# Holding back the load of batch 1's x until the first piece of batch 0's x has landed

## The chip, the core and the metric

The kernel runs on one core of a Trainium2 chip. The metric is the device time of one execution in microseconds (us); the time of the kernel before is 225.44 us, the median of 3 runs (225.27 to 225.44).

The core has five engines with instruction queues of their own, each in order: TensorE (PE in the profile; its weight loads are listed apart as PEld), VectorE (DVE), ScalarE (ACT), GpSimd (POOL) and SyncE (SP), which here only issues transfers. Transfers between the chip's memory and the on-chip memory are carried out by 16 DMA engines. Transfers issued by SP go through the queue that the profile calls q1, those issued by ACT through q10, and those issued by POOL through q0.

## The reference

```python
# x: (8, 8, 512, 64), state: (8, 8, 32, 64); B, H, S, D and Ns = 32
scores = scale * np.matmul(x, state.transpose(0, 1, 3, 2))
a = softmax(scores)                        # over the 32 states
xread = np.matmul(a, state)
scores2 = scale * np.matmul(state, x.transpose(0, 1, 3, 2))
a2 = softmax(scores2)                      # over the 512 tokens
sread = np.matmul(a2, x)
h = concatenate([xread, sread], axis=2)    # then (batch, position) x (head, D) = 4352 x 512
gate = 1 / (1 + np.exp(-(h @ w_gate)))     # 512 x 1536
val = h @ w_val
out = (gate * val) @ w_out                 # 1536 x 512
```

## The kernel before

The work goes batch by batch (8 batches of x). For a batch, x arrives as 32-bit floats in the tile `xf` (128 partitions x 8 heads x 4 x 64; 1 MB), is cast to bfloat16 (`xb`), is transposed (`xT`), and is multiplied with the state for the scores (`S_mm`). ACT takes the exponentials (`S_exp`), DVE sums the rows (`n_sum`, line 139) and inverts the sums, the normalized scores (`ab`) are transposed (`aT`), and the product with `SW` (the state times the two input weights) gives gate and value (`gv_mm`, line 288). A tanh on ACT and a product on DVE make `glu`, and `out_mm` (line 319) multiplies by the output weight. The second attention (`sr_mm`, `sr_fin`) shares the exponentials; its results `XS` are collected and go through the feed-forward part last.

The order of the instructions on each engine is the order in which the code is written (`manual_schedule`): batches 0 and 1 are interleaved by hand from line 392 on, the others follow in a loop. An engine whose next instruction waits holds up everything written for it further down. The change works in the first 11 us of the hand-written part. What stands there, in the order of the code:

- `load_s(0)` (line 392) issues the state of batches 0 and 1 on ACT; `load_x(0, nc.sync, 4)` (line 393) issues x of batch 0 on SP in four transfers of two heads each, 256 KB; `load_x(1, nc.sync, 4)` (line 394) does the same for batch 1, with no wait. The next thing on SP is a DMA transpose much later.
- POOL: makes the identity matrix, casts heads 0 and 1 of batch 0 (line 404), casts the state (`cast_s`), issues three weight transfers of 256 KB, then `gate` (line 431), a copy of one element per partition that waits for heads 6 and 7 of batch 0 and so holds back the further weight transfers; then two of these, the cast of heads 6 and 7 of batch 1 (line 445), and `at_Eb` (line 132), a cast of the exponentials.
- DVE: fills constants, casts heads 2 and 3 of batch 0 (line 406), copies the padded state and the transposed x out of PSUM (lines 382 and 108), casts heads 2 and 3 of batch 1 (line 429), casts heads 4 and 5 of batch 1 (line 439), and then sums the rows (`n_sum(0, 1)`, line 440). From there to `sr_fin(0)` (line 476) it goes on with sums, reciprocals, copies and products of both batches.
- ACT: casts heads 6 and 7, then 4 and 5 of batch 0 (lines 413 and 416), with a copy of a transposed tile, casts heads 0 and 1 of batch 1 (line 436), and takes the exponentials (`S_exp(0, 1)`, line 438).
- PE: runs matmuls on constants (`warm`) while it waits, transposes x, and computes scores. `aT_mm(1, OU)` (line 483) writes to the PSUM tile that `sr_fin(0)` on DVE has to leave first.

All casts of x stand at line 91 in the profile, all transfers of x at line 74.

Of the kernel before, what the change touches and what calls it, by code (L numbers as in the profile page):

```python
# [8 lines left out]
FP = mybir.dt.float32  # L9
# [7 lines left out]
def kernel(  # L17
# [14 lines left out]
    nc = tc.nc  # L32
    B, H, S, D = x.shape
# [10 lines left out]
    stg = ctx.enter_context(tc.tile_pool(name="stg", bufs=3))  # L44
# [20 lines left out]
    xfs, xbs, xTs = {}, {}, {}  # L65
# [2 lines left out]


    def load_x(b, eng, parts=1):  # L70
        xf = xfs[b] = stg.tile((128, H, 4, D), FP, name="xf")
        v, n = x[b].rearrange("h (p c) d -> p h c d", c=4), H // parts
        for i in range(parts):
            eng.dma_start(xf[:, n * i:n * i + n], v[:, n * i:n * i + n])  # L74

    def load_w(w, lo, n):
        src = (moe_w_gate, moe_w_val)[w].rearrange("(k p) n -> p k n", p=128)
        nc.gpsimd.dma_start((wg, wv)[w][:, :, lo:lo + n], src[:, :, lo:lo + n])
# [9 lines left out]
    def cast_x(b, cp, lo, n):  # L88
        if b not in xbs:
            xbs[b] = xp.tile((128, 4, H, D), BF, name="xb")  # L90
        cp(xbs[b].rearrange("p c h d -> p h c d")[:, lo:lo + n], xfs[b][:, lo:lo + n])  # L91
# [257 lines left out]
    def warm(n, place):  # L349

        ps = place[0].tile((128, 512), FP, name="warm", tag=place[1])
        for _ in range(n):
            nc.tensor.matmul(ps[:, :128], ones[:, 0], ones[:, 0], start=True, stop=True)  # L353
# [37 lines left out]

    load_s(0, nc.scalar)
    load_x(0, nc.sync, 4)
    load_x(1, nc.sync, 4)
    make_identity(nc, ident)
    for e in range(2):
        nc.vector.memset(ones[:, e, e * 64:e * 64 + 64], 1.0)
# [3 lines left out]
    pre = wp.tile((128, 2), FP, name="pre")  # L401
    nc.scalar.activation(pre[:, 0:1], ones[:, 0, 0:1], AF.Exp)

    cast_x(0, pool, 0, 2)
    warm(12, OU)
    cast_x(0, vec, 2, 2)
# [105 lines left out]
    load_sb(3)  # L512
    load_sb(1)
    load_x(2, nc.gpsimd, 2)
    p_tok(1)
    sw_cp(1, 1024, 0, 1, act)
# [221 lines left out]
```

## Time and profile before

| what | us |
|---|---|
| median of 3 runs | 225.44 |
| the profiled execution | 226.03 |
| its span, first to last instruction | 224.2 |
| PE busy | 217.0 |
| DVE busy | 140.7 |
| ACT busy | 127.6 |
| POOL busy | 48.8 |

The durations in the text come from the one profiled execution. The span is what lies between its first and its last instruction; some 1.8 us lie around it. All times of the trace count from the start of the span.

A line of a group in the profile names the line of the code, the engine, the operation, what it writes and reads (output <- inputs, shapes), and how often; then busy time, mean duration of one in ns, and how long the engine stood idle before these instructions and for whom. A line of the timeline gives start and duration in us, engine, line, operation, tiles and count, and in brackets the idle time before it with what ended it. The chain of waits follows the work that ended last back to what released it, and lists the pieces in order of time. A line on transfers gives what was loaded, the issuing engine, count, size of one, and the median time from issue to landing.

### The profile page before, as it was taken

The page shows a single profiled execution, that of the slowest core. Times are in us where ns is not written, and L with a number is a line of the kernel's source. Part 1 is how long each engine was busy: PE and PEld are TensorE (multiplying, and loading weights), DVE is VectorE, ACT ScalarE, POOL GpSimd, SP SyncE. Part 2 cuts the span into 40 slices and gives each one's busy share as a digit, 9 for nine tenths or more (in the row PEclk, how much of TensorE's full clock was granted, in tenths as well). Part 3 has the DMA queues.
Part 4 walks back from the last instruction along what each step waited for, and adds up shares of the span by engine and source line. Part 5 has one row for each costly group of instructions (what it writes and reads, how often), then busy time and mean ns, then how long its engine had stood idle before and what let it go on. Part 6 is the DMA issues. An engine that isn't in the chain of part 4 may idle for free.

```text
span 224.2 us, 4791 instructions
## 1 busy us (share of the span) xinstructions
PE 217.0 (97%) x1859; PEld 111.2 (50%) x1859; DVE 140.7 (63%) x248; ACT 127.6 (57%) x239; POOL 48.8 (22%) x85
## 2 busy tenths in 40 slices
PE   7789999999999999999999999999999999999994
PEld 6654444444444545454444454454445444466744
DVE  3599897779368756885488648864787434422311
ACT  2587885645676557656675667556755444423311
POOL 3799560362041004200240006000200000000001
PEclk9999999999999999999999999999999999999999
DMA  6999989753898352627362521253122111111114
GB/s 188 289 201 206 280 130 179 114 193 78 147 292 274 71 151 76 219 59 126 100 225 50 121 96 61 44 81 117 47 78 66 50 50 47 67 73 48 50 26 114
DMA packets 38566, 27.37 MB, mean 122 GB/s; under 512 B 21168, under 2 KB 33840, under 8 KB 38544
## 3 DMA queue, kind: packets, MB, share of 16 engines
q1 hardware_dynamic: 31392, 19.74, 32.5%
q0 software_dynamic: 6864, 7.14, 17.6%
q8 instruction: 14, 0.23, 0.4%
q10 hardware_dynamic: 288, 0.20, 0.3%
q14 instruction: 8, 0.07, 0.1%
HBM read 18.35 MB, written 8.91 MB: 122 GB/s over the span
## 4 chain that ended last, share of the span: by engine, by line
PE 91%; DVE 3%; DMA 2%; ACT 1%; SPq 1%; issue 0%
PE outp L319 38%; PE gvp L288 37%; PE swp L236 5%; PE gvp L291 5%; DMA xf<-in_x_dram 2%; PE srp L213 1%; PE Sp L121 1%; PE outp L339 1%; DVE rs L139 1%; PE srp L210 1%; SPq L74 1%; DVE ab L173 1%; DVE ri L141 0%; DVE r L218 0%; PE xTp L105 0%; PE warm L353 0%
## 5 line engine op out<-in xcount | busy, mean ns | idle before, releaser
L303 DVE SCALAR_TENSOR_TENSOR glu<-th,gvp 128x512 bf16<-128x512 f32 (+1 forms) x108 | 69.9, 655 | 64.0 <-ACT th L298 48.7
L319 PE MATMUL outp<-wo,glu 128*128 128x512 bf16 x396 | 98.2, 379 | 0.0
L288 PE MATMUL gvp<-aT,SW 128*128 128x512 bf16 x384 | 96.3, 379 | 0.3 <-DVE aT L190 0.2
L298 ACT ACTIVATE th<-gvp 128x512 f32<-128x512 f32 (+1 forms) x108 | 61.8, 574 | 60.6 <-PE gvp L288 49.2
L288 PEld LDWEIGHTS <-SW 128*128 128x128 bf16 x384 | 36.3, 98 | 44.7 <-issue 3.1
L319 PEld LDWEIGHTS <-glu 128*128 128x128 bf16 x396 | 37.4, 98 | 40.8 <-issue 0.4
L274 ACT CAST SW<-swp 128x512 bf16<-128x512 f32 x70 | 38.8, 586 | 4.7 <-PE swp L236 3.3
L132 POOL CAST Eb<-E 128x256 bf16<-128x256 f32 x32 | 11.5, 407 | 89.9 <-ACT E L126 89.9
L323 ACT ACTIVATE res<-outp 128x512 f32<-128x512 f32 x33 | 19.7, 597 | 17.6 <-PE outp L319 17.6
L274 DVE CAST SW<-swp 128x512 bf16<-128x512 f32 x26 | 17.1, 683 | 1.6 <-PE swp L236 1.4
L91 POOL CAST xb<-xf 128x1024 bf16<-128x1024 f32 (+1 forms) x13 | 13.8, 1093 | 12.1 <-DMA xf<-in_x_dram 10.7
L330 POOL DMA_DIRECT2D out_dram<-res x2 | 1.1, 542 | 60.0 <-ACT res L323 60.0
L147 DVE TENSOR_REDUCE E<-E 128x128 f32<-128x512 f32 x12 | 12.4, 1035 | 0.0
L139 DVE TENSOR_REDUCE rs<-E 128x16 f32<-128x512 f32 x16 | 10.8, 676 | 1.3 <-ACT E L126 1.3
L126 ACT ACTIVATE E<-Sp 128x512 f32<-128x512 f32 x16 | 9.6, 604 | 2.4 <-PE Sp L121 2.4
L173 DVE TENSOR_TENSOR ab<-E,ri 128x512 bf16<-128x512 f32 x12 | 9.6, 804 | 0.0
L236 PE MATMUL swp<-wg,sTc 64*32 64x512 bf16 (+1 forms) x192 | 8.4, 328 | 0.0
L236 PEld LDWEIGHTS <-sTc 64*32 64x32 bf16 x384 | 4.5, 91 | 7.4 <-issue 4.7
L218 DVE RECIPROCAL r<-srp 128x128 f32<-128x128 f32 x8 | 7.6, 950 | 0.0
L121 PEld LDWEIGHTS <-xT 128*128 128x128 bf16 x128 | 5.5, 98 | 4.0 <-DVE xT L108 1.0
L236 PE MATMUL swp<-wv,sTc 64*32 64x512 bf16 (+1 forms) x192 | 7.4, 322 | 0.0
L291 PE MATMUL gvp<-XS,wg 128*128 128x256 bf16 x48 | 7.2, 273 | 0.0
(64 smaller groups left out, 122.0 us busy)
## 6 DMA issues: line engine op xcount, KB each, us to landing
out_dram<-res SPq DMA_DIRECT2D x31, 256.0 KB, 2.6
xf<-in_x_dram SPq DMA_DIRECT2D x12, 256.0 KB, 4.5
xf<-in_x_dram SPq DMA_DIRECT2D x3, 1024.0 KB, 6.8
wo<-in_moe_w_out_dram POOLq DMA_DIRECT2D x3, 512.0 KB, 5.9
wg<-in_moe_w_gate_dram POOLq DMA_DIRECT2D x2, 512.0 KB, 9.2
wv<-in_moe_w_val_dram POOLq DMA_DIRECT2D x2, 512.0 KB, 10.8
xf<-in_x_dram POOLq DMA_DIRECT2D x2, 512.0 KB, 10.4
xf<-in_x_dram POOLq DMA_DIRECT2D x1, 1024.0 KB, 9.2
```

The source lines that it names most:

```text
L91: cp(xbs[b].rearrange("p c h d -> p h c d")[:, lo:lo + n], xfs[b][:, lo:lo + n])
L139: nc.vector.tensor_reduce(rs, halfE(b, i), AX.X, ALU.add)
L147: nc.vector.tensor_reduce(held["E4", b][:, e].rearrange("p j n -> p (j n)"), E1s[b][:, :, e].rearrange("p c j n -> p (j n) c"), AX.X, ALU.add)
L173: eng.tensor_tensor(abs_[b].rearrange("p c e (j n) -> p (c e) j n", n=Ns)[:, ce, 2 * i:2 * i + 2], halfE(b, i)[:, ce], ri[:, ce].unsqueeze ...
L236: nc.tensor.matmul(pss[e][j * Ns:(j + 1) * Ns, o:o + n], sTc[rows, b, j] if b > 1 else sTz[rows, b, j, e], (wg, wv)[w][rows, j, lo:lo + n] ...
L274: cp(*sw_left.pop((b, lo, w, e)))
L288: nc.tensor.matmul(ps, SWs[b][:, g, w, fs], aTs[b][:, :, g], start=(g == 0), stop=(g == 1))
L291: nc.tensor.matmul(ps, (wg, wv)[w][:, j, fs], XS[:, j], start=(j == 0), stop=(j == 3))
L298: nc.scalar.activation(th, held["gv", b, f][0], AF.Tanh, scale=0.5)
L303: nc.vector.scalar_tensor_tensor(glus[b][:, f], held["th", b, f], 1.0, held["gv", b, f][1], ALU.add, ALU.mult)
L319: nc.tensor.matmul(ops[b, c], glus[b][:, f, c * 128:(c + 1) * 128], wo[:, f], start=(f == 0), stop=(f == NF - 1))
L323: nc.scalar.activation(res, ops[b, c], AF.Copy, scale=0.5)
```

## The change

`load_x` no longer makes its tile if it exists already. A new helper, `hold_x(b, a)`, makes the tile for batch b and lets POOL copy one element per partition of batch a's tile into it. Since the element belongs to heads 0 and 1 of batch a, the copy waits for the first transfer of batch a; and since it writes where the first transfer of batch b is going to write, SP waits for the copy before it issues this transfer. The load of batch 1 is moved behind the constants, follows `hold_x(1, 0)`, and is cut in two transfers of four heads, 512 KB each, where it was cut in four. The copy stands on POOL ahead of the cast of heads 0 and 1 of batch 0. The casts and all that follows stand in the order in which they stood.

```diff
     def load_x(b, eng, parts=1):
-        xf = xfs[b] = stg.tile((128, H, 4, D), FP, name="xf")
+        if b not in xfs:
+            xfs[b] = stg.tile((128, H, 4, D), FP, name="xf")
+        xf = xfs[b]
         v, n = x[b].rearrange("h (p c) d -> p h c d", c=4), H // parts
         for i in range(parts):
             eng.dma_start(xf[:, n * i:n * i + n], v[:, n * i:n * i + n])
+
+    def hold_x(b, a):
+
+        xfs[b] = stg.tile((128, H, 4, D), FP, name="xf")
+        nc.gpsimd.tensor_copy(xfs[b][:, 0, 0, 0:1], xfs[a][:, 0, 0, 0:1])
...
     load_s(0, nc.scalar)
     load_x(0, nc.sync, 4)
-    load_x(1, nc.sync, 4)
     make_identity(nc, ident)
...
     nc.scalar.activation(pre[:, 0:1], ones[:, 0, 0:1], AF.Exp)
 
+    hold_x(1, 0)
+    load_x(1, nc.sync, 2)
     cast_x(0, pool, 0, 2)
```

## The prediction

> **What bounds the kernel now.** The page's first two parts say that TensorE (PE) is the bound, but not evenly. The columns are busy time, share of the span, instructions; in the second row one digit is 5.6 us.
>
> ```profile
> PE 217.0 (97%) x1859; PEld 111.2 (50%) x1859; DVE 140.7 (63%) x248; ACT 127.6 (57%) x239; POOL 48.8 (22%) x85
> ...
> PE   7789999999999999999999999999999999999994
> ```
>
> PE has holes in the first four slices only. I asked next for PE's waits from 18 us to the end: the answer lists none. So from 18 us on PE cannot make up what it loses before, and what the change does to the moment at which that stretch begins is what it does to the end, nearly one for one. The edit works in the first 11 us, so I read the chain of waits from 7 to 18.6 us (start, length, what):
>
> ```profile
> 2.27 5.24 DMA xf<-in_x_dram
> ...
> 7.53 0.63 ACT xb L91
> ...
> 10.09 0.60 ACT E L126
> ...
> 10.71 0.70 DVE rs L139
> ...
> 17.55 0.30 DVE XS L226
> 17.85 0.04 issue
> 17.90 0.61 PE aTp L180 x8
> ```
>
> The chain starts at the last quarter of batch 0's x (issued at 2.27, landed at 7.51), goes through ACT's cast, transposes and scores to the exponentials at 10.09, and from 10.71 to 17.85 it lies on VectorE (DVE) without a gap. DVE is strictly in order, so whatever starts the row sums at 10.71 (line 139) sets the end. The timeline shows what stands ahead of them:
>
> ```profile
> 4.22 0.61 POOL L91 CAST xb<-xf 128x512 bf16<-128x512 f32 x1 [2.91 <-DMA xf<-in_x_dram]
> ...
> 9.12 0.62 ACT L91 CAST xb<-xf 128x512 bf16<-128x512 f32 x1
> ...
> 9.50 0.75 DVE L91 CAST xb<-xf 128x512 bf16<-128x512 f32 x2
> ...
> 10.38 0.62 POOL L91 CAST xb<-xf 128x512 bf16<-128x512 f32 x1 [1.22 <-DMA xf<-in_x_dram]
> 10.71 0.69 DVE L139 TENSOR_REDUCE rs<-E 128x16 f32<-128x512 f32 x1 [0.46 <-ACT E L126]
> ```
>
> The casts at 9.12 and later are batch 1's. On DVE the cast of heads 4 and 5 of batch 1 (line 439) stands right before the row sums (line 440); now it is done at 10.25 and DVE then waits 0.46 us for ACT. The only cast of batch 1 that waits for its data is POOL's, of the last quarter, which is there at 10.38.
>
> **The change, part by part.**
> *The copy.* One more POOL instruction of one element per partition. The nearest row is the gate's copy (line 82): 0.19 us. It waits for batch 0's first quarter, for which POOL's cast at 4.22 waits anyway, so it adds no wait on POOL, but everything behind it moves by 0.19: that cast, the state's cast (4.78), the weight transfers (from 5.12), the gate (7.56). The cast feeds PE and DVE, which then idle 1.23 us until 8.21 and 2.05 us until 9.16: hidden. Of the weights, the first that PE waits for is wait-bound by 0.2 us at 15.92, and its work is not on the chain, which is DVE's there: hidden, and if not, 0.2.
>
> *The issue on SP.* Eight issues of about 0.47 us each become four, a wait, and two. Now batch 1's go out from 2.78 to 4.79. After: the quarter lands at 4.2, the copy runs from 4.22 to 4.41, SP wakes at about 4.45 (an estimate: 0.04 after its releaser, as in its other rows), issues the halves at 4.45 and 4.95. The next thing on SP is a transpose at 31.68, so nothing behind the wait suffers.
>
> *When batch 1 lands.* This is the disputed number. Now its four quarters are issued at 2.78 to 4.3 and take 5.5, 5.7, 5.9 and 6.0 us, since they stand in line behind batch 0; the last is there at 10.3. After, 1 MB is issued from 4.45. The trace has no 1 MB in two halves, so I bound it by the nearest rows. Above: 1 MB in one transfer, issued at 86.44 and at 59.41, took 6.6 and 6.8 us (a third took 9.0, among output stores). Near: batch 7's x in four quarters, issued from 110.03; its last quarter, issued about 112.1, took 4.0, so 6.1 us from the first issue. Below: the first quarter alone takes 3.4, and if the other 768 KB followed at the 367 GB/s that the windows show from 3 to 4 us, that is 3.4 + 2.1 = 5.5 us. So batch 1 is complete between 4.45 + 5.5 = 9.95 and 4.45 + 6.8 = 11.25. I take 6.25, between the two nearest rows (6.1 and 6.6) and nearer to the one that is cut in pieces: 10.7.
>
> Why it isn't just as early as now: now the 2 MB run through one queue without a break. After, batch 0's data is almost through when batch 1's halves are issued, and a transfer of this queue moves nothing for its first 1.4 us (issued at 0.74; the windows show 15 GB/s up to 2.00), then ramps up: after the issue at 110.03, 47 GB/s in 111.5 to 112.0, 332 in the next microsecond.
>
> *What that costs.* Heads 4 to 7 now come as one piece. DVE's cast of heads 4 and 5 can start 0.05 after the landing and takes 0.42, the row sums start 0.02 later: 10.7 + 0.49 = 11.19 in place of 10.71, so **+0.48 us**. POOL's cast of heads 6 and 7 moves from 10.38 to 10.75 and its next work (line 132) from 11.23 to about 11.4; POOL's part of the chain ends at 17.44, some 0.4 us before DVE's, so this hides. The first half must be there for ACT's cast at 9.12, behind which the exponentials wait; they need it by 9.4. One quarter takes 3.4 and a second 0.7 more at full rate, so 8.6; with the stop that batch 0 shows between its second and third quarters (3.6 and 5.0 us to landing, for issues half a microsecond apart) 1 us later, 9.6. That is 0.2 us late at most, and in parallel with the 0.48, not added.
>
> *What batch 0 gains.* Its last two quarters take 5.0 and 5.2 us with four more queued behind them; batch 7's, with none behind, took 3.8 and 4.0. If batch 1's queueing is the reason, the last quarter lands at 6.3 to 6.8 and not 7.51, and ACT's casts, the transposes and the scores come some 0.7 us earlier. But the row sums would still stand behind the cast of heads 4 and 5, so DVE waits for batch 1 instead of for ACT: the gain goes into idle time. The Trainium skill (DMA: Bandwidth & Descriptors, "Queues, rings and completion order") says that the descriptors of a queue are consumed in ring order on each DMA engine, so what is queued behind should not slow what is ahead. By it batch 0 keeps its 7.51 and no gain exists at all; the rows of 4.0 against 5.2 speak against it, though batch 7's quarters met other traffic. The chance of a gain below is lower for it.
>
> *Sum.* +0.48 us on DVE, the other edits hidden, and PE after 18 us passes it on. The profiled execution took 226.03 us (span 224.2 and 1.83 around it), 0.59 over the median of the runs, 225.44; the difference is put onto the median: 225.44 + 0.5 = **225.95**.
>
> **The rivals.** A difference under 0.2% (0.45 us) is about what a measurement of this kernel can't tell from no change.
>
> *Hidden (0.33).* Batch 1's data needs no break if batch 0's stragglers keep the DMA engines busy until its descriptors come. Then it lands as now, at 10.3, or up to 10.6: the cast and the row sums at 10.8 to 11.1, +0.1 to +0.4. For it: batch 0's last landing is 7.51, 1.7 us after the first data of batch 1 can flow (4.45 + 1.4 = 5.85). Against it: the windows show 289 and 288 GB/s in 2 to 4 and 4 to 6 us, 1.15 MB by 6.0, and batch 0 with the state is 1.18 MB; so by then nearly all of batch 0 is through, what lands at 7.51 is the tail of a few DMA engines, and the rest would stand idle. Time 225.45 to 225.85.
>
> *Faster (0.16).* Batch 0's last quarter lands 0.7 us earlier and batch 1's two halves flow at the full rate. The mechanism sits at line 439: if batch 1 is complete by 9.75, the cast is done at 10.22 and the row sums start at 10.25 in place of 10.71. The bottom of my bound, 9.95, gives 10.44, -0.27; the point from which it is faster by 0.45 is 9.75, just under that. ACT allows it (its path would be ready at 10.71 - 0.7 = 10.0). Time 224.7 to 225.0. The same page of the Trainium skill ("Anatomy of one DMA") gives about 2.0 us fixed plus the bytes over 436 GB/s; by that, an estimate, 1 MB from 4.45 is complete at about 8.9, and this case would hold. The 6.6 and 6.8 us of the 1 MB rows, where it gives 4.4, speak against it.
>
> *Slower, the forecast (0.51).* Landing from 10.65 to 11.3 and later: +0.45 to +1.1, 225.9 to 226.5. Its worst form is the stop of some 1.1 us seen between batch 0's quarters falling on batch 1's second half.
>
> *The edit doesn't do what it says.* The listing of the changed program's instructions shows the copy ahead of POOL's first cast, SP's wait on POOL ahead of the fifth transfer, and no other order changed on PE; so no chance of its own.
>
> **How the numbers follow.** The forecast 225.95 is of the likeliest case. The range leaves out half of the faster case and the tail of the slower: 225.0 to 226.6. Faster by over 0.2%: 0.16; within: 0.33; slower: 0.51.
>
> **What would show it.** In the changed kernel's profile: a POOL copy of 0.19 us at 4.2; SP's fifth transfer at 4.4 to 4.5, the first half landing 4.1 to 5.1 us after its issue and the second 5.5 to 6.0; DVE idle before its cast at line 91, ended by DMA, in place of 0.46 us before line 139 ended by ACT; the first row sums at about 11.2; PE's aTp transposes at about 18.4 in place of 17.90. It is wrong if batch 1's last half lands before 9.9, or if the first row sums move and PE's start at 17.90 doesn't.

## The result, and the profile after

The changed kernel takes 229.4 us (median of 6 runs, 228.1 to 229.86) against 225.36 for the kernel before: a ratio of 1.0166, with a 95% interval of 1.0145 to 1.0187. The medians lie 4.0 us apart. The forecast was 225.95, in a range up to 226.6: the sign held, the size didn't. Ratios leave out executions that took over 1.5% longer than the fastest of their kernel (two of ten with the shorter wait below and three of ten with the other order on VectorE, all with a fallen clock); medians keep them.

The profiled execution has a span of 228.1 us against 224.2. First the page: its busy row of PE, PE in 40 slices, and the row that hardly mattered before, the clock that TensorE was granted.

```profile
PE 218.6 (96%) x1834; PEld 113.2 (50%) x1859; DVE 141.2 (62%) x248; ACT 127.8 (56%) x239; POOL 49.0 (21%) x86
...
PE   7679999999999999999999999999999999999994
...
PEclk9967999999999999999999999999999999999999
```

PE's holes are where they were, but in the third and fourth slice (11.4 to 22.8 us) the clock falls to 6 and 7 tenths; in the profile before, all of this row was 9. Next the chain of waits of the changed kernel up to 22 us (start, length, what), to be held against the one from 7.51 to 17.90 before:

```profile
6.12 9.27 DMA wg<-in_moe_w_gate_dram
15.39 0.04 issue
15.44 0.63 PE swp L243 x11
16.07 0.97 PE srp L217 x8
17.03 0.85 PE srp L220 x16
17.89 0.87 PE aTp L187 x8
18.75 0.02 issue
18.78 0.59 ACT aT L197
...
21.36 0.61 PE aTp L187 x8
```

DVE has left the chain between 12 and 19 us; PE itself stands there. The second transposes of `ab` start at 21.36 in place of 17.90, 3.46 us later, and the PE instructions behind them keep just this distance to their partners before until about 60 us; another 0.24 comes there and 0.14 at the very end, which makes the 3.84 between the two spans (228.06 and 224.22). The timeline shows how it begins (line 98 is the cast of x, line 146 the row sums):

```profile
4.18 0.19 POOL L81 COPY xf<-xf 128x1 f32<-128x1 f32 x1 [2.88 <-DMA xf<-in_x_dram]
...
6.51 1.14 ACT L98 CAST xb<-xf 128x512 bf16<-128x512 f32 x2 [3.82 <-DMA xf<-in_x_dram]
...
10.40 0.62 ACT L98 CAST xb<-xf 128x512 bf16<-128x512 f32 x1 [2.20 <-DMA xf<-in_x_dram]
...
11.07 0.62 PE L112 MATMUL xTp<-ident,xb 128*128 128x128 bf16 x8 [1.81 <-ACT xb L98]
11.76 0.43 DVE L98 CAST xb<-xf 128x512 bf16<-128x512 f32 x1 [0.99 <-DMA xf<-in_x_dram]
11.79 0.87 POOL L98 CAST xb<-xf 128x512 bf16<-128x512 f32 x1 [2.54 <-DMA xf<-in_x_dram]
12.10 0.68 DVE L146 TENSOR_REDUCE rs<-E 128x16 f32<-128x512 f32 x1
...
15.44 0.41 PE L243 MATMUL swp<-wg,sTz 64*32 64x256 bf16 x8 [0.34 <-DMA wg<-in_moe_w_gate_dram]
...
17.70 1.04 PE L187 MATMUL aTp<-ident,ab 128*128 128x128 bf16 x8
```

Batch 0's last quarter is there at 6.5, a full microsecond earlier than before. But every cast of batch 1 now waits for its data, DVE's first and ACT's until 10.34 and 10.40, DVE's second and POOL's until 11.76 and 11.79, and the row sums start at 12.10 in place of 10.71: **1.39 us**. PE meanwhile has nothing for 1.81 us. What follows stands in the windows (after the colon: PE's, PEld's, DVE's, ACT's, POOL's busy time, then the clock). Before:

```profile
9.20:12.60 3.40, 2.67 (x48) 2.03 (x45) 2.87 (x8) 2.58 (x6) 1.98 (x6) 1.00 1.43 198
12.60:16.00 3.40, 2.92 (x88) 2.24 (x88) 3.33 (x9) 2.87 (x7) 3.40 (x6) 1.00 1.36 203
```

After:

```profile
9.20:12.60 3.40, 1.04 (x15) 0.67 (x12) 1.27 (x3) 1.60 (x3) 0.85 (x2) 1.00 1.26 176
12.60:16.00 3.40, 2.61 (x38) 1.53 (x37) 3.33 (x9) 2.27 (x4) 3.40 (x9) 0.50 1.42 200
16.00:19.40 3.40, 3.40 (x72) 2.96 (x64) 1.34 (x5) 1.69 (x4) 3.40 (x5) 0.50 1.26 204
```

PE works 1.04 us of the 3.4 before 12.6, where it worked 2.67, and from 12.6 to 19.4 it runs at half its clock. At that rate PE becomes the bound: the eight transposes of `ab` at 17.70 take 1.04 us, where their partners before took 0.61:

```profile
14.66 0.61 PE L180 MATMUL aTp<-ident,ab 128*128 128x128 bf16 x8
```

From the row sums (+1.39) to the transposes at 21.36 (+3.46) it loses **2.07 us** more. The theory to be tested was therefore: the wait makes batch 1's x late, which costs 1.4 us on DVE's path, and the hole that this opens on PE takes the clock down, which costs 2 (theory A). Rivals: the late weights of the chain's first line cost the rest, and the clock is only a sign (B); the coarse halves, not the wait, are late (C); and for the lateness itself, weights beside it (D) or its own slow transfers (E).

### The profile page after: what moved, and what is told of

Its sections match the earlier page's. It is cut to its first block, busy times and chain, and to the rows that moved or that the text cites. A ratio compares the mean times of both kernels' runs of the same rounds, so it can differ in the third digit from the quotient of the medians.

```text
span 228.1 us, 4765 instructions
## 1 busy us (share of the span) xinstructions
PE 218.6 (96%) x1834; PEld 113.2 (50%) x1859; DVE 141.2 (62%) x248; ACT 127.8 (56%) x239; POOL 49.0 (21%) x86
## 4 chain that ended last, share of the span: by engine, by line
PE 90%; DMA 6%; DVE 1%; POOL 1%; issue 1%; ACT 1%; ACTq 0%
PE outp L326 37%; PE gvp L295 37%; PE swp L243 5%; PE gvp L298 5%; DMA wg<-in_moe_w_gate_dram 4%; PE srp L220 2%; DMA xf<-in_x_dram 1%; PE outp L346 1%; PE srp L217 1%; PE Sp L128 1%; PE aTp L187 1%; DVE r L225 0%; POOL wv L85 0%; ACT res L330 0%; ACT aT L197 0%
## 5 line engine op out<-in xcount | busy, mean ns | idle before, releaser
L326 PE MATMUL outp<-wo,glu 128*128 128x512 bf16 x371 | 95.3, 379 | 1.3 <-issue 0.2
L139 POOL CAST Eb<-E 128x256 bf16<-128x256 f32 x32 | 11.4, 403 | 89.4 <-ACT E L133 89.4
L146 DVE TENSOR_REDUCE rs<-E 128x16 f32<-128x512 f32 x16 | 10.8, 676 | 0.9 <-ACT E L133 0.9
## 6 DMA issues: line engine op xcount, KB each, us to landing
wg<-in_moe_w_gate_dram POOLq DMA_DIRECT2D x2, 512.0 KB, 10.6
wv<-in_moe_w_val_dram POOLq DMA_DIRECT2D x2, 512.0 KB, 11.7
```

Of the source, the lines that this page charges most:

```text
L139: nc.gpsimd.tensor_copy(Ebs[b][:, c], E1s[b][:, c])
L146: nc.vector.tensor_reduce(rs, halfE(b, i), AX.X, ALU.add)
L326: nc.tensor.matmul(ops[b, c], glus[b][:, f, c * 128:(c + 1) * 128], wo[:, f], start=(f == 0), stop=(f == NF - 1))
```

## The experiments

Times are ratios to the kernel before on the same chip, with a 95% interval where there are enough runs.

### The parts of the change: two halves without the wait, the wait with four quarters, the copy alone

```diff
-    load_x(1, nc.sync, 4)
+    load_x(1, nc.sync, 2)        # the kernel before, nothing else
```

> The kernel before with x of batch 1 in two transfers of 512 KB, issued at once as before; no copy, no wait. Theory A (the wait breaks the stream of transfers, the cut in two is harmless): both halves land as their last quarters did, about 9.0 and 10.3 us; 225.2 to 225.8 us. Rival C (the coarse halves are what comes late, since a half is usable only with its last DMA engine): row sums at 11.5 us or later, 226.5 us or more.

```diff
     hold_x(1, 0)
-    load_x(1, nc.sync, 2)
+    load_x(1, nc.sync, 4)        # the changed kernel
```

> The changed kernel with x of batch 1 in four transfers of 256 KB behind the same wait. Theory A: the first quarters land earlier than the first half did (10.3), about 8.5 and 9.5, the last at about 11.7 still; row sums near 11.3 to 11.8 because they stand behind the third quarter; TensorE's hole is smaller, the clock may or may not hold: 226.3 to 229. Rival C (halves): 225.9 or less.

```diff
+    gate(xfs[0][:, 0, 0, 0:1])   # the kernel before
     cast_x(0, pool, 0, 2)
```

> The kernel before with one more copy of one element on GpSimd at the place where the change puts it, into a tile that nothing waits for; x of batch 1 is issued as before. Theory A and the prediction: the copy's 0.19 us are hidden, within 0.2% of the kernel before. Rival B (the copy's shift of the weight transfers is what costs): 226.5 us or more.

Two halves at once: 1.0025 (1.0002 to 1.0047). The wait with four quarters: 230.24 us, 1.0209 (1.0176 to 1.0242), if anything worse than with two. The copy alone: 1.0007 (0.9982 to 1.0031). So the wait is the cost; the cut adds a little, the copy nothing that can be told from no change, and rival C falls. The numbers expected for the four quarters were too low: the last one landed not at 11.7 but at 13.25.

### Why the held x is late: no weights beside it

```diff
-    load_w(1, 256, 256)   load_w(0, 256, 256)   load_w(0, 0, 256)
...
-    gate(xfs[0][:, 7, 0, 0:1])
+    gate(xfs[1][:, 7, 0, 0:1])
+    load_w(1, 256, 256)   load_w(0, 256, 256)   load_w(0, 0, 256)
```

Of the changed kernel (two halves), and of the one with four quarters:

> The changed kernel with all weight transfers held on GpSimd until the last half of x of batch 1 has landed. Read for the landing, not for the time, which the late weights must raise. Theory D (held back, x of batch 1 shares the DMA engines with the weights, which flow from 8.7 us on, and a few engines finish late): no weights beside it, the last half lands at 10.0 to 10.6 us. Theory E (the lateness is the transfer's own: pause, slow start and stragglers): it still lands at 11.5 or later.

> x of batch 1 in four quarters behind the wait (as in the run whose last quarter landed at 13.25 us, 9.0 us after the first issue), with all weight transfers held on GpSimd until that last quarter has landed. A second pair for the same question; read for the landing, the time must rise. Theory D (weights beside it are what makes the held x late): last quarter 6.0 to 6.6 us after the first issue, near 10.5. Theory E (its own stragglers): 7.3 us or more after it.

The transfer rows of the last piece of batch 1 (last column: us from its issue to its landing). The changed kernel, and the same with the weights behind:

```profile
xf<-in_x_dram SPq DMA_DIRECT2D x1, 512.0 KB, 6.9
```

```profile
xf<-in_x_dram SPq DMA_DIRECT2D x1, 512.0 KB, 5.7
```

Four quarters held, and the same with the weights behind:

```profile
xf<-in_x_dram SPq DMA_DIRECT2D x1, 256.0 KB, 7.6
```

```profile
xf<-in_x_dram SPq DMA_DIRECT2D x1, 256.0 KB, 4.2
```

Counted from the first issue of batch 1 to the last landing, it is 7.3 us against 6.1 with halves, and 9.0 against 5.6 with quarters. The halves landed at 10.8, a little over the 10.6 that theory D allowed and well under the 11.5 of theory E; the quarters at 10.2, even sooner after their first issue than the 6.0 us of theory D. Two more executions with the changed kernel's halves and weights beside them (below) took 8.3 and 7.0 us. So with weights beside it the held x came 1.2 us later in one pair and 3.4 in the other, which bears D out; each member of a pair is a single profiled execution. Both kernels are slower (232.72 and 231.09 us): their weights come later still, and their clock falls too, with halves for 10.2 us.

The piece is not late as a whole. In the changed kernel 15 of the 16 DMA engines have finished their share of the last half at 10.3 us and one at 11.73; the cast waits for that one. Not all of this is the weights': with the weights behind, 15 engines have finished the last half at 9.67 us and the last one at 10.79. Why single engines fall behind stays open.

### A shorter wait

```diff
-        nc.gpsimd.tensor_copy(xfs[b][:, 0, 0, 0:1], xfs[a][:, 0, 0, 0:1])
+        nc.gpsimd.tensor_copy(xfs[b][:, 0, 0, 0:1], sfs[a][:, 0, 0, 0:1])
```

> The changed kernel with the copy taken from the state's tile, which landed at 3.54 us, so that SP issues the two halves at about 3.8 instead of 4.4. A smaller dose of the same wait. If the lateness grows with the wait (the pause before the first data, 1.4 us or more from the issue, is no longer covered by data of batch 0): the last half lands at about 10.5 to 11.2, row sums at about 11.0 to 11.7, 226 to 228.5 us. If any wait breaks the stream as badly: as the changed kernel, 228 to 230.

226.31 us, 1.0038 (1.0014 to 1.0062). SP issues at 3.86 in place of 4.40, and the last half lands at 10.2, 0.3 us before what was expected and 1.5 before the changed kernel's; the row sums of the profiled execution start at 10.56. Half a microsecond less of waiting takes away three quarters of the loss. Here too there are weights beside the held x, yet it takes only 6.3 us from the first issue to the last landing: from 8.5 us on SP's queue has only 0.10 MB left to move, against 0.30 MB in the changed kernel, and the first weights flow at 8.4 and 8.9 us. Its ten executions fall into groups: seven with a mean granted clock of 0.998 or more have spans of 224.0 to 224.8, one at 0.992 has 225.2, and two at 0.985 have 227.5 and 228.1. How late x was in the last two is not known, as the profiled execution is one of the seven; their 3 to 4 us need not be the clock's alone.

### The clock: more matmuls in the hole, and fewer in the kernel before

```diff
     S_exp(0, 0)
+    warm(26, GV)                 # the changed kernel
     xT_mm(1, 0, SWP)
```

> The changed kernel with 26 more matmuls on constants (1.7 us by the rows of the earlier ones, 67 ns each) where TensorE waits for x of batch 1. Theory A (the late x costs 1.4 us on VectorE's path, and the hole that it opens on TensorE takes TensorE's clock to half for 6.8 us, which costs the rest): granted clock 1.00 after 12 us, row sums still at about 12.1 us, 226.5 to 227.2 us. Rival B (the cost comes from the late weight transfers, the clock is only a sign of the waiting): clock back at 1.0, but the time stays at 228.5 or more.

```diff
-    warm(15, GV)   warm(3, GV)   warm(3, GV)   warm(6, GV)    # the kernel before
```

> The kernel before without its 27 matmuls on constants between 6 and 9.6 us; transfers untouched. Prices the clock alone. Theory A (low activity of TensorE takes the clock to half for some 6.8 us, and this stretch is worth 1 to 2.5 us): granted clock 0.5 in a stretch after 10 us, 226.4 to 228. Rival (the clock follows only from the waits for data and costs nothing by itself): 225.2 to 225.7.

The first is not the test that it should have been: 229.87 us, 1.0196 (1.0141 to 1.025). In two of its four executions the clock still fell (0.989 and 0.985, spans 229.3 and 228.8), in two it didn't (1.0 and 0.997, spans 227.2 and 226.9). Those two took 229.03 and 228.71 us. By the time alone that is what rival B expected (clock back, 228.5 or more), and theory A's 226.5 to 227.2 was missed. The profiled execution is one of the two, and shows where its time went. The last half came even later there:

```profile
12.53 0.43 DVE L98 CAST xb<-xf 128x512 bf16<-128x512 f32 x1 [1.84 <-DMA xf<-in_x_dram]
...
12.87 0.68 DVE L146 TENSOR_REDUCE rs<-E 128x16 f32<-128x512 f32 x1
```

and in its chain of waits

```profile
4.60 7.90 DMA xf<-in_x_dram
...
12.96 0.61 DVE rs L146
...
20.05 0.61 PE aTp L187 x8
```

The row sums are 2.16 us late (12.87 for 10.71) and the transposes 2.15 (20.05 for 17.90). The chain between them lies on DVE, behind the last half of x, with no weights on it. At full clock the lateness of the row sums passes on one for one, and nothing is added; in the changed kernel 1.39 became 3.46. The last computation is 2.15 us late as well; the span, 2.9 us longer than before, has its other 0.8 in the last stores of the output. So the time that looks like rival B's comes from x, which landed 0.8 us later than in the changed kernel, and from the stores. In the changed kernel the late weights do show: PE waits 0.34 us for `wg`, which lands at 15.39, and up to that much of the 2.07 may be theirs. A run with the weights early and x late was not made.

The kernel before with fewer constants: 227.48 us, 1.0079 (1.0048 to 1.0111), that is 1.8 us (1.1 to 2.5) with transfers untouched. Its profile has no clock row, but its matmuls tell it:

```profile
15.72 1.06 PE L213 MATMUL srp<-Eb,xb 128*128 128x64 bf16 x16
16.59 0.94 PE L180 MATMUL aTp<-ident,ab 128*128 128x128 bf16 x8
```

0.63 and 0.61 in the kernel before. The low stretch is not the same one as in the changed kernel: it has begun by 8.25 us, where transposes of x are slow already, and moves the row sums by 0.45. The other six executions, not profiled, give its price by its depth: mean clocks of 0.991 and 0.992 go with spans of 224.4 and 224.7, 0.984 and 0.985 with 225.6 and 225.7, two of 0.977 with 226.1 and 226.3, while the kernel before has 223.6 to 223.7 at its median. A mean of 0.984 is what the changed kernel has in its profiled execution, with its 6.8 us at half clock. So a drop of that depth costs about 2.0 us with the transfers untouched, close to the 2.07 found above.

### The order on VectorE

```diff
-    cast_x(1, vec, 4, 2)
     n_sum(0, 1)
+    cast_x(1, vec, 4, 2)         # the changed kernel
```

> The changed kernel with VectorE's first row sums of batch 0 ahead of its cast of heads 4 and 5 of batch 1. If the prediction's step holds (that cast is what the row sums wait for), they start right after the exponentials, at about 11.5 us instead of 12.10, still bound by the first half of x through ScalarE's cast; the gain on the end is at most 0.6 us, since the transposes of batch 1 come as late as before, and the clock still drops: 228 to 229.6. If the row sums don't move, something else held them.

```profile
11.58 0.69 DVE L146 TENSOR_REDUCE rs<-E 128x16 f32<-128x512 f32 x1 [0.78 <-ACT E L133]
```

The row sums go ahead and wait for ACT's exponentials, as expected; the cast behind them is at 12.47. 228.29 us, 1.0105 (1.0068 to 1.0143): part of the loss, not more, since the transposes of batch 1 are as late as before: DVE's second row sums come at 13.86, 1.98 us late, and the second transposes of `ab` at 19.88, late by the same. The clock fell in five of the ten executions, to 0.985 in four (spans 227.7 to 228.3) and 0.992 in one; the others have 224.4 to 226.7.

### Versions without the wait

Two halves with 8 more matmuls ahead of `xT_mm(1, 2, AT)`; three transfers (heads 0 to 3, 4 and 5, 6 and 7); three transfers with 6 more matmuls there:

```diff
-    load_x(1, nc.sync, 4)
+    load_x(1, nc.sync, (4, 2, 2))   # heads of each transfer
```

> x of batch 1 in two transfers issued at once, without copy or wait, and 8 more matmuls on constants in TensorE's hole ahead of the transposes of heads 4 and 5 of batch 1. If the dropped clock (in some executions) was what made the two halves 0.25% slower: clock 1.00 in all runs and 225.0 to 225.5 us, level with the kernel before. If not: 225.6 to 226.0 still.

> x of batch 1 issued at once in three transfers, heads 0 to 3, then 4 and 5, then 6 and 7. Heads 4 and 5, which VectorE's path waits for, then needn't wait for 6 and 7. If the wait for a whole half is what two halves cost: row sums at 9.8 to 10.2 us, 224.6 to 225.3. If not: 225.5 to 226.

> The three transfers together with 6 more matmuls on constants ahead of the same transposes. If both causes count, the fastest of all: 224.4 to 225.2 us with clock 1.00; if neither, as the kernel before or slower by the matmuls' 0.4 us.

1.0035 (1.0007 to 1.0063), 0.9994 (0.9973 to 1.0015) and 0.9994 (0.9973 to 1.0014). With three transfers the row sums of the profiled execution start at 9.59, 1.1 us before those of the kernel before, and wait for ACT, not for data. Still the median doesn't differ: the profiled execution of before, 226.03 us, was one of its longer ones, so part of that distance is that one execution's. And in the profiles of all three versions the row sums have left the chain that leads to the second transposes of `ab`: it comes from a weight transfer (`wv`, issued at 7.60 and landed at 15.48 with three transfers), so x still earlier would find the weights in its way. The two halves stay a third of a per cent slower at full clock too (0.998 or more in all twelve executions), so the clock is not what they cost; what is, stays open. None beats the kernel before.

## Why the prediction was wrong

- *What bounds the kernel, and that DVE's start at line 139 sets the end:* right under a condition that it did not name, PE at full clock. There 2.16 us on the row sums gave 2.15 on PE, and moving them in DVE's order moved them to ACT's exponentials. Towards earlier it ends at the weights: row sums 1.1 us earlier, with three transfers, left the median where it was. That PE passes on what it has lost by 18 us held: 3.46 us at 21.36 became 3.84 at the end.
- *The copy is hidden:* right, 1.0007 with the copy alone.
- *SP issues the halves at 4.45 and 4.95:* right, 4.40 and 4.81.
- *Batch 0 lands at 6.3 to 6.8 and the gain goes into idle time:* right. It landed at 6.5, and PE then had a hole of 1.81 us.
- *Batch 1 complete at 10.7, 6.25 us from the issue:* the term that was mis-sized. It took 7.3, over the upper bound of 6.8; in other executions with the same wait and weights beside it 7.0 to 9.0. The 1.39 us that this put on the row sums would alone have given 226.8, just over the range. The rows chosen as nearest (6.1 and 6.6 us) had no weights beside them, and without weights the held halves take 6.1 and start the row sums at 11.15, where the forecast had 11.19 (they were issued 0.2 us later there, so the last digit is chance). The prediction moved the weights by 0.19 us and asked what their delay would cost; it did not ask what they would do to the x that was pushed in among them, though the windows of before show the DMA share going from 1.06 to 1.25 at 8.5 us. The Trainium skill (DMA: Bandwidth & Descriptors, "Issuing engines are not separate DMA queues") says that transfers of all issuers run on the same 16 DMA engines and interleave. The pairs above agree: 5.7 against 6.9 us, and 4.2 against 7.6.
- *The first half at 8.6 to 9.6, at most 0.2 late:* wrong, 10.3; with the weights behind it came at 9.4, inside the range. It didn't set the row sums, but it made the hole on PE.
- *Whatever starts the row sums "sets the end", and so the sum, 0.48 us and nothing else:* the step that failed by most. Between the row sums and the transposes at 17.90 it took PE's rate as given. A hole of PE was put at nothing because DVE was on the chain, and the clock was not looked at. What the runs showed in its place is 2.07 us of the 3.46, of which late weights may hold up to 0.34; the rest goes to PE at half clock, by the chain and by the price of the drop without a change in transfers. (The sum as it is written, 225.44 + 0.5, is 225.94.)
- *The estimate of 8.9 us in the faster case:* the figure stands in the Trainium skill (DMA: Bandwidth & Descriptors, "Anatomy of one DMA") in a section on transfers that GpSimd issues, and SP issues x. No held batch 1 was complete before 10.2.
- *The rivals:* the forecast case named its worst form, a straggler on the second half, at 226.5. A straggler did come: with the weights beside it the held last piece landed at 11.7 us (halves) and 13.25 (quarters). The clock's fall on top of it stood in none of the cases, so that the likeliest case had the right sign is to the credit of the lateness alone.

## What to carry to other kernels

Before a transfer is held back, look at what flows when it will flow: its duration has to come from rows with that company, and the piece counts as landed with its last DMA engine. And before a hole on TensorE is called free because another engine is on the path, look at whether the activity that is left keeps its clock. Here it didn't: for 6.8 us matmuls took 1.4 to 1.7 times as long (0.41 against 0.30 us for eight of `swp`, 1.04 against 0.61 for eight transposes), and TensorE became the path.

## What the runs showed of the hardware

- The clock fell to half without any long pause: the longest hole of PE ahead of the fall at 12.6 was 1.81 us, with 1.04 us busy in the 3.4 us before it. The Trainium skill (TensorE: Matmul & The Clock Gate, "Part 1: The HAM clock gate") speaks of half rate after an idle window of some 3.4 us; here a window with some work in it was enough. What the threshold is stays open, and PE's busy time alone does not tell it: with two halves and no wait the clock fell at 13.1 us after 3.4 us with 2.23 busy, while 1.94 us busy from 10.03 to 13.45 in the execution with 26 more matmuls, and 1.90 from 9.78 to 13.20 in the one with the other order on VectorE, went without a fall.
- The fall is a matter of the execution as well as of the kernel: with the shorter wait it came in three executions of ten.
- In all three profiles with eight transfers of 256 KB queued at once, of the kernel before or with its transfers, the last quarter of batch 0 landed at 7.16 to 7.55 us; in all eleven with batch 1 held or in fewer pieces it landed at 6.38 to 6.73. It is not the bytes behind it: the same 1 MB queued at once in two or three pieces gave 6.38 to 6.59. So the prediction's conclusion that what is queued behind should not slow what is ahead does not hold for these eight pieces; in each, one or two DMA engines end it 0.5 to 0.9 us after the others (after 6.63, 6.66 and 6.76 us), and the reason is open.
